# Attention and two MoE layers on one core: the first batch of heads visited twice, and the first MoE block let in earlier

## The chip, the cores and the metric

The kernel runs on one NeuronCore of a Trainium2 chip. The metric is device time of one execution in microseconds (us); smaller is better. Engines are named PE (TensorE matmul), PEld (its weight load), DVE (VectorE), ACT (ScalarE), POOL (GpSimd) and SP (SyncE, which here only issues transfers, one after the other in program order).

## The reference, cut to what matters

Attention over 4 batches, 8 heads, 576 positions of 64 numbers, with a threshold on the scores, then two dense "expert" layers on the 2304 tokens of 512 numbers:

```
scores = (q @ k.T) / 8
thresh = max(scores, axis=-1) - tau
scores = where(scores >= thresh, scores, -1e9)
attn   = exp(scores - max(scores)); attn /= sum(attn) + 1e-9
x      = (attn @ v)                        -> 2304 tokens x 512
layer 1: h = x @ w_in (512 x 2048); g = elu(h);        y = g @ w_out (2048 x 512)
layer 2: h = y @ w_in (512 x 2048); g = max(0.01h, h); y = g @ w_out (2048 x 512)
```

All inputs are float32 and so is the accuracy that is wanted. A product is formed in one of two ways: in plain fp32 on PE, or "split": each operand is written as a high and a low part in the type fp32r, and PE forms high*high, low*high and high*low.

## The kernel before, in words

**Pairs and units.** Two neighbouring heads of one batch make a pair (16 pairs, 4 to a batch), and their 1152 query rows are cut into nine units of 128 rows: A0 to A3 of the even head, B0 to B3 of the odd one, and M, which holds the last 64 rows of both. `ORDER` (L38) is the order in which a pair's units are taken. One unit does: two halves of q.k into a PSUM tile (L488 in fp32, L495 split), the copy to SBUF with the row minimum (DVE, L503), the threshold (L506 or L508), the mask and the exponential on ACT (L512, L515), four PE transposes of the weights (L528) and one shared by two units (L565). The transposed weights are copied out of PSUM by 128 rows at a time: for an fp32 product by two plain copies (`wh`, `lt`, L585 and L587, recorded at L617 on ACT or L618 on DVE), for a split product by a cast on ACT (L595, L602) and a subtraction on DVE (L598, L605) for each of the two. When a head's window of 256 rows (w = 0: units 0 and 1) or 320 rows (w = 1: units 2, 3 and half of M) is full, its attn.v product is formed (`pv32`, L636: five fp32 matmuls; `pv`, L655: nine split ones) and copied into `x` (L641; L661 and, for the split form, a DVE addition, L662). After the ninth unit the row sums are transposed (L538), inverted (L539), sent through DRAM and back (L540, L544), and `x` of that pair is scaled (`scaled`, L550).

**Which heads are fp32.** `Q32` = 4 and `P32` = 9: heads 0 to 3 form q.k, and heads 0 to 8 attn.v, in fp32. An fp32 head has only k, q and v loaded (L404, L405, L392). A split pair goes through `kq_pair` (L417): one load each of the raw k and q of both heads, four POOL operations that split them (L308, L304), and twelve SBUF-to-SBUF transfers (L438) that put the parts where PE wants them. The raw and high tiles have one buffer, `k1` and `k2` two (one for each head of a pair), the q tiles one for each head of a pair. v of a split head is split by two POOL operations (L397 to L399).

**MoE blocks beside the attention.** Layer 1's first half of the hidden dimension (8 slices of 128) is computed for six blocks of 256 tokens while attention runs (`beside`, L835), into the PSUM banks `h` and `y`. Block i needs the scaled `x` of all four pairs of the batches that its tokens lie in (`block_deps`, L831). Each of its eight steps is 12 matmuls of `step_h` (L696) and 12 of `step_y` (L737). The 16 weight tiles that these steps need are loaded (L261) and split on POOL, DVE and ACT at a pace set by `wv0` and `wv1`. While the bank pair is free of blocks (`early`, the first `NS` = 41 units), every second unit's scores go to bank `y` and the shared transpose to `h`; after that all scores go to the one tile `s`. After the 144th unit attention's memory is given back, the second half of layer 1's weights is loaded, and the rest (layer 1's other blocks, then layer 2) runs.

**Order.** All instructions are first listed with their dependences, a cost, and a due time (`vt`): a unit's is its number times `TU`, to which `ST0` (the first `U0` units) or `ST1` adds an offset for each kind of operation; block i's is `bs[i]` times `TU`, and `bdt` for each step. A planner (`Order.run`) then walks through time and puts on each engine, among the operations that its cost model holds ready, the one with the smallest due time. That gives a fixed order for each engine and for SP; on the chip every engine goes through its order and waits where an operand isn't there. SP's model has no bandwidth: 600 ns for each issue, and a latency.

Of the kernel before, what the change touches and what calls it, by code (L numbers as in the profile page):

```python
# [20 lines left out]
NH = B * H  # L21
P32, Q32 = 9, 4
# [15 lines left out]
ORDER = ("A0", "A1", "A2", "A3", "M", "B2", "B3", "B0", "B1")  # L38
COLS = ("A0", "A1", "A2", "A3", "M", "B0", "B1", "B2", "B3")
# [7 lines left out]
ST0 = dict(qk=-10184.2, max=-1817.2, thr=14955.0, exp=-1497.1, mask=5372.6, rec=-38303.7, norm=-27876.4,  # L47
           tr=-1492.3, hi=-17426.6, lo=-14703.9, lhi=28901.5, llo=26005.4, pv=-66898.0)
ST1 = dict(qk=-17406.0, max=4726.7, thr=-9260.7, exp=-6889.7, mask=-5170.3, rec=10649.6, norm=11088.8, tr=5091.6,
           hi=-37131.6, lo=5775.7, lhi=-970.1, llo=-7799.8, pv=-16488.8)  # L50
# [162 lines left out]
def mm32(n):  # L213
    return 2 * (3 + n / 1.2)
# [3 lines left out]
def attn_moe_kernel(ctx, tc, qT, kT, vm, tau, w1i, w1o, w2i, w2o, yp, rsd, out):  # L218
# [36 lines left out]
    def weight(layer, which, f, vt, after=(), reg=False):  # L255
# [6 lines left out]
                after, [raw], vt - 4000, lat=4500)  # L262
# [124 lines left out]
    def head(g, u):  # L387
        vt = (u - KN["hleadb" if g % 2 else "hlead"]) * TU
        par = g % 2
        if g < P32:  # L390
            v = v_r.new(F32)
            ov = op((SP, 600, lambda: nc.sync.dma_start(out=v()[:, :, 0:D], in_=vm[g])), [], [v], vt + KN["vlate"],  # L392
                    lat=3000)
        else:
            vr, v = vraw_r.new(), v_r.new()
            hi, lo = (lambda: v()[:, :, 0:D]), (lambda: v()[:, :, D:2 * D])
            lv = op((SP, 600, lambda: nc.sync.dma_start(out=vr(), in_=vm[g])), [], [vr], vt - 3000, lat=3000)  # L397
# [3 lines left out]
        if g < Q32:  # L401
            k, q = k1_r.new(F32), k2_r.new(F32)
            due = vt - (3e3 if g else 3e4)
            lk = op((SP, 600, lambda: nc.sync.dma_start(out=k()[0:64], in_=kT[g])), [], [k], due, lat=3000)  # L404
            lq = op((SP, 600, lambda: nc.sync.dma_start(out=q()[0:64, 0:S], in_=qT[g])), [], [q], due, lat=3000)  # L405
            heads[g] = (k, k, q, v, (lk, lq), ov)
            if "tau" not in heads:
                heads["tau"] = load_tau(vt)
            return
# [3 lines left out]
        heads[g] = (k1, k2, q, v, deps, ov)  # L413
# [3 lines left out]
    def kq_pair(p, vt):  # L417
# [4 lines left out]
        for r, h, src, n in ((kr, kh, kT, SL), (qr, qh, qT, S)):  # L422
            ld = op((SP, 600, lambda r=r, src=src: nc.sync.dma_start(
                out=r(), in_=src[2 * p:2 * p + 2].rearrange("g d s -> (g d) s"))), [], [r], vt - 3000, lat=3500)
# [5 lines left out]
        for j in range(2):  # L430
# [3 lines left out]
            for dst, at, cs, src, raw, o in (  # L434
# [5 lines left out]
                    [o], [src, dst], vt + 1500 + 5 * TU * j, lat=3000))  # L440
# [6 lines left out]
    def unit(u, p, name):  # L447
# [23 lines left out]
        def er(n=S):  # L471
            return e()[:, side, 0 if side or n > S else 1:n if side or n > S else S + 1]

        def ssr(n=S):
            return ss()[:, 1:S + 1] if n == S else ss()[:, side:side + S + 1]

        nm, thr = (sm_r[t].new() for t in ("nm", "thr"))
        n9 = u % NU
        if n9 == 0:
            sums[p] = (su_r.new(), [])  # L480
        su, col = sums[p][0], COLS.index(name)
        hd = [heads[pc[0]] for pc in pieces]

        def qk32(j):
            for n, (g, c, _, _, w) in enumerate(pieces):
                k, _, q = heads[g][:3]
                c -= 64 if g % 2 and name != "M" else 0
                nc.tensor.matmul(s()[n * w:n * w + w, j, 0:HALF], q()[0:64, c:c + w],  # L488
                                 k()[0:64, k0 + j * HALF:k0 + (j + 1) * HALF], start=True, stop=True)

        def qk(j):
            for n, (g, c, *_) in enumerate(pieces):
                k1, k2, q = heads[g][:3]
                for m, kk in enumerate((k1, k2)):
                    nc.tensor.matmul(s()[:, j, 0:HALF], q()[:, c:c + 128], kk()[:, k0 + j * HALF:k0 + (j + 1) * HALF],  # L495
                                     start=(n == 0 and m == 0), stop=(n == len(pieces) - 1 and m == 1))
# [3 lines left out]
        cost, fn = (mm32(HALF), qk32) if q32 else (2 * mm(HALF), qk)  # L500
# [16 lines left out]
        sums[p][1].append(o)  # L517
        if n9 == NU - 1:
            row_sums(p, vt + so["rec"])
# [11 lines left out]
        turned.append((vt, pieces, t4, t, ott, o, side))  # L531
# [3 lines left out]
    def row_sums(p, vt):  # L535

        (su, done), rb, rt, ps = sums.pop(p), rb_r.new(), rt_r.new(), v_ps.new()
        o = op((PE, 107, lambda: nc.tensor.transpose(ps()[0:NU, 0:128], su(), ident)), done, [su, ps], vt)  # L538
        o = op((DVE, dve(128), lambda: nc.vector.reciprocal(out=rt(), in_=ps()[0:NU, 0:128])), [o], [ps, rt], vt)  # L539
        o = op((SP, 600, lambda: nc.sync.dma_start(out=rsd[p].rearrange("(c p) -> c p", p=128), in_=rt())),  # L540
               [o], [rt], vt, lat=2500)
        got = []
        for a, c, r, n in ((0, 0, 0, S), (64, 0, S + 64, 512), (64, 512, S, 64)):
            got.append(op((SP, 600, lambda a=a, c=c, r=r, n=n: nc.sync.dma_start(  # L544
                out=rb()[a:a + 64, c:c + n], in_=rsd[p, r:r + n].partition_broadcast(64))), [o], [rb], vt, lat=3000))
# [25 lines left out]
    def weights(vt, pieces, t4, t, ott, _, side, lv, otl, so):  # L571
        l0 = 64 * side
        c0 = 0
        for g, _, w, c, n in pieces:
# [9 lines left out]
            if f32:  # L584
# [5 lines left out]
                if full:  # L590
                    pv32(g, w, vt + so["pv"])
# [335 lines left out]
```

## Time and profile before

| | |
|---|---|
| Time, median of 3 runs | 1123.71 us (1123.56 to 1124.15) |
| Profiled execution | 1122.48 us, of which 1120.7 us are the span of its instructions |
| Instructions | 17435 |
| Granted TensorE clock | 1.000 over the span |
| PE: chain that ended last | 91% of the span; DVE 5%, ACT 3% |
| First q.k matmul on PE | 6.4 us |
| Last inversion of row sums of the first batch | 121.3 us |
| First matmul of a MoE block | 138.0 us |
| Last inversion of row sums, end of attention | 443.3 us |

The first 443 us are attention with the six blocks beside it; the remaining 677 us are matmuls of the two layers almost alone. A matmul's recorded length overlaps the next one's, so a matmul's cost is read as the distance from its start to the start of what follows it. An fp32 matmul leaves two records.

### The profile page before, as it was taken

To read this page: it belongs to the slowest core of one execution; us is meant where nothing else is said; L and a number is where in the kernel's file an instruction comes from. 1 tells how busy PE (TensorE), PEld (TensorE's weight loads), DVE (VectorE), ACT (ScalarE), POOL (GpSimd) and SP (SyncE) were. 2 spreads that over 40 slices of the span, in tenths; PEclk is the share of its full clock that TensorE was granted. 3 is DMA by queue.
4 is the path that set the end of the run, shared out by engine and by line. 5 is a ranking of instruction groups with operands and counts; after the bars stand their busy time and mean duration, and the time that the engine had idled before them with its cause. 6 is when DMAs were issued, how large, how long until landed. Compare 5 with 4: busy or idle time off the path is not lost.

```text
span 1120.7 us, 17435 instructions
## 1 busy us (share of the span) xinstructions
PE 1103.0 (98%) x6328; PEld 932.4 (83%) x6328; DVE 712.3 (64%) x1467; ACT 622.3 (56%) x1315; POOL 285.0 (25%) x385
## 2 busy tenths in 40 slices
PE   8999999999999999999999999999999999999998
PEld 4455589999999999889888888988888888888898
DVE  6677798889888887578787784866432332332232
ACT  6778789998888897555455453544322322222232
POOL 4355567565636552012111020100000000000000
PEclk9999999999999999999999999999999999999999
DMA  6466645545454531323442330322010010010010
GB/s 183 112 164 151 168 134 131 160 115 132 115 133 114 132 93 40 95 76 121 143 131 76 113 116 17 114 75 75 1 38 1 1 38 1 1 38 1 1 39 19
DMA packets 50645, 95.45 MB, mean 85 GB/s; under 512 B 13168, under 2 KB 20864, under 8 KB 50560
## 3 DMA queue, kind: packets, MB, share of 16 engines
q1 hardware_dynamic: 50560, 94.34, 29.9%
q8 instruction: 50, 0.82, 0.3%
q14 instruction: 35, 0.29, 0.1%
HBM read 58.20 MB, written 9.51 MB: 60 GB/s over the span
## 4 chain that ended last, share of the span: by engine, by line
PE 91%; DVE 5%; ACT 3%; issue 1%; DVEq 0%; ACTq 0%
PE y L737 34%; PE h L696 19%; PE hb L696 15%; PE v L636 5%; PE s L495 5%; PE v L655 5%; PE t L528 5%; DVE ss L503 1%; ACT e L515 1%; PE s L488 1%; DVE rt L539 1%; PE y L495 1%; PE y L488 1%; DVE wl L598 1%; ACT ss L512 1%
## 5 line engine op out<-in xcount | busy, mean ns | idle before, releaser
L737 PE MATMUL y<-gh,woh 128*128 128x512 f32 (+1 forms) x736 | 257.2, 349 | 1.3 <-DVE ys L618 0.9
L737 PE MATMUL y<-gl,woh 128*128 128x512 f32 (+1 forms) x736 | 252.5, 343 | 0.0
L737 PE MATMUL y<-gh,wol 128*128 128x512 f32 (+1 forms) x736 | 252.2, 343 | 0.0
L696 PE MATMUL h<-xh,wih 128*128 128x256 f32 (+1 forms) x464 | 158.8, 342 | 1.0 <-DVE g L714 1.0
L737 PEld LDWEIGHTS y<-gh,woh 128*128 128x128 f32 x736 | 139.1, 189 | 18.6 <-DVE ys L618 1.4
L696 PE MATMUL h<-xh,wil 128*128 128x256 f32 (+1 forms) x464 | 153.2, 330 | 0.0
L696 PE MATMUL h<-xl,wih 128*128 128x256 f32 (+1 forms) x464 | 153.1, 330 | 0.0
L737 PEld LDWEIGHTS y<-gl,woh 128*128 128x128 f32 x736 | 139.2, 189 | 16.2 <-DVE gl L303 0.2
L737 PEld LDWEIGHTS y<-gh,wol 128*128 128x128 f32 x736 | 139.0, 189 | 16.3
L721 ACT CAST gh<-g 128x512 fp32r<-128x512 f32 (+1 forms) x184 | 97.0, 527 | 91.2 <-DVE g L719 49.0
L512 ACT ACTIVATE ss<-ss,thr 128x576 f32<-128x576 f32 x144 | 111.7, 776 | 19.8 <-DVE thr L508 13.4
L303 DVE TENSOR_TENSOR gl<-g,gh 128x512 fp32r<-128x512 f32 (+1 forms) x129 | 84.2, 652 | 52.8 <-ACT gh L721 51.7
L515 ACT ACTIVATE e<-ss,taun 128x577 f32<-128x577 f32 x144 | 112.2, 779 | 2.5 <-PE h L565 0.8
L503 DVE TENSOR_SCALAR_CACHE_REDUCE ss<-s,scl 128x576 f32<-128x576 f32 x124 | 100.6, 811 | 19.9 <-PE s L495 7.9
L304 POOL TENSOR_TENSOR xl<-x,xh 128x256 fp32r<-128x256 f32 (+1 forms) x32 | 27.9, 884 | 290.3 <-ACT xh L674 290.3
L696 PE MATMUL hb<-xh,wih 128*128 128x512 f32 (+1 forms) x272 | 99.1, 364 | 0.0
L495 PE MATMUL s<-k,qt 128*128 128x288 f32 x512 | 97.8, 302 | 1.3 <-DVE ss L503 1.1
L696 PE MATMUL hb<-xl,wih 128*128 128x512 f32 (+1 forms) x272 | 99.1, 364 | 0.0
L696 PE MATMUL hb<-xh,wil 128*128 128x512 f32 (+1 forms) x272 | 99.0, 364 | 0.0
L696 PEld LDWEIGHTS h<-xh,wih 128*128 128x128 f32 x464 | 87.5, 189 | 10.2 <-ACT lt L602 0.8
L696 PEld LDWEIGHTS h<-xl,wih 128*128 128x128 f32 x464 | 87.7, 189 | 8.5 <-POOL xl L304 0.2
L696 PEld LDWEIGHTS h<-xh,wil 128*128 128x128 f32 x464 | 87.5, 189 | 8.1
(538 smaller groups left out, 1959.8 us busy)
## 6 DMA issues: line engine op xcount, KB each, us to landing
k<-kh SPq DMA_DIRECT2D x56, 160.0 KB, 2.5
k<-kraw SPq DMA_DIRECT2D x56, 160.0 KB, 2.9
wraw<-in_w1i_dram SPq DMA_DIRECT2D x16, 512.0 KB, 3.5
wraw<-in_w1o_dram SPq DMA_DIRECT2D x16, 512.0 KB, 3.5
wraw<-in_w2i_dram SPq DMA_DIRECT2D x16, 512.0 KB, 3.6
wraw<-in_w2o_dram SPq DMA_DIRECT2D x16, 512.0 KB, 3.4
kraw<-in_kT_dram SPq DMA_DIRECT2D x14, 320.0 KB, 3.1
ys<-yp_dram SPq DMA_DIRECT2D x4, 1024.0 KB
```

What stands on the lines that cost most here:

```text
L303: return pick(who, D=(dve(n), lambda: nc.vector.tensor_tensor(**args()), PORT), P=(pool_tt(n), lambda: nc.gpsimd.tensor_tensor(**args())))
L304: P=(pool_tt(n), lambda: nc.gpsimd.tensor_tensor(**args())))
L495: nc.tensor.matmul(s()[:, j, 0:HALF], q()[:, c:c + 128], kk()[:, k0 + j * HALF:k0 + (j + 1) * HALF], start=(n == 0 and m == 0), stop=(n == ...
L503: o = op((DVE, dve(S) + 60, lambda: nc.vector.tensor_scalar(out=ssr().rearrange("p (j c) -> p j c", j=2), in0=s()[:, :, 0:HALF], scalar1=s ...
L512: o = op((ACT, act(S) + 95, lambda: nc.scalar.activation(out=ssr(), in_=ssr(), func=AF.Prelu, bias=thr(), scale=-1.0, alpha=STEEP)), [ot], ...
L515: o = op((ACT, act(S) + 190, lambda: nc.scalar.activation(out=er(S + 1), in_=ssr(S + 1), func=AF.Exp, bias=taun, accum_out=su()[:, col:col ...
L528: nc.tensor.transpose(t4()[:, c, :], er()[:, c1 + c * 128:c1 + (c + 1) * 128], ident)
L636: nc.tensor.matmul(ps()[0:64, 0:nw], lhs, rhs, start=(c == 0), stop=(c == 4))
L655: nc.tensor.matmul(ps()[:, 0:nw], vv()[:, c, :], y()[:, yc, 0:nw] if yc is not None else y()[:, 0:nw], start=(n == 0), stop=(n == 8))
L696: nc.tensor.matmul(hp(), w_()[:, cs], x_()[:, 0:tb], start=(k == 0 and z == 0), stop=(k == KC - 1 and z == 2))
L721: o1 = op((ACT, act(tb), lambda: nc.scalar.copy(out=gh()[:, cs], in_=g()[:, cs])), [o], [g, gh], vt)
L737: nc.tensor.matmul(ysl(yg, m), w_()[:, cs], g_()[:, 0:tb], start=(first and z == 0 and share == 0), stop=(last and z == 2 and end))
```

## The change

The first batch's four pairs are taken in two visits instead of one. `FIRST` does the units A0, A1, B0, B1 of all four pairs (16 units, the first 256 rows of each head, tokens 0 to 255 of the batch), `SECOND` the units A2, A3, M, B2, B3 (20 units, the last 320 rows), and the other twelve pairs are done as before (`ALL`). Each visit loads k, q and v of its heads anew and has its own row sums and its own scaling of `x`; `block_deps` now looks at ranges of tokens, so that block 0 (tokens 0 to 255) needs only the four FIRST visits.

fp32 is left to FIRST: q.k of all eight heads (`Q32` = 20, but only there), attn.v of heads 0 to 4 (`P32` = 5). All SECOND and ALL visits are split. The due times are new: block 0's and block 1's move from 46.325 and 62.85 units to 19.686 and 40, the weights' pace from 4.28 to 3.78 units for a tile, scores leave bank `y` after 16 units instead of 41, and `pv32`'s five matmuls are one operation of the planner.

```diff
-P32, Q32 = 9, 4
+P32, Q32 = 5, 20
-ORDER = ("A0", "A1", "A2", "A3", "M", "B2", "B3", "B0", "B1")
-U0 = H // 2 * NU
-KN = dict(margin=49.6784, pad=30.0, late=1.30757, plead=2.02161, warm=3, TU=2594.9, hlead=-1.09928,
-          hleadb=1.51858, wv0=3.7208, wv1=4.27865, yoff=32778.1, coff=-7939.5, NS=41, vlate=-5075.7,
-          bs=[46.325, 62.85, 80.6, 98.984, 114.51, 134.31], bdt=1.91944, look=0.128169)
+ALL = (("A0", "A1", "A2", "A3", "M", "B2", "B3", "B0", "B1"), ("A0", "A1", "A2", "A3", "M", "B0", "B1", "B2", "B3"),
+       (0, S), ((0, 0, 0, S), (64, 0, S + 64, 512), (64, 512, S, 64)))
+FIRST = (("A0", "A1", "B0", "B1"),) * 2 + ((0, 256), ((0, 0, 0, 256), (64, 0, 256, 256)))
+SECOND = (("A2", "A3", "M", "B2", "B3"),) * 2 + ((256, S), ((0, 0, 0, 320), (64, 0, 384, 256), (64, 256, 320, 64)))
+PLAN = [(p, kind) for kind in (FIRST, SECOND) for p in range(H // 2)] + [(p, ALL) for p in range(H // 2, NH // 2)]
+U0 = H // 2 * len(FIRST[0])
+KN = dict(margin=31.666, pad=0, late=1.30757, plead=2.29704, warm=3, TU=2578.7, hlead=-1.2502, hleadb=1.94318,
+          wv0=3.66401, wv1=3.77649, yoff=31272.0, coff=-12887.2, NS=16, vlate=-1115.6,
+          bs=[19.686, 40, 74.316, 88.029, 111.03, 127.05], bdt=1.92668, look=0.259586)
...
-        if g < P32:
+        if kind is FIRST and g < P32:
             v = v_r.new(F32)
...
-        if g < Q32:
+        if kind is FIRST and g < Q32:
             k, q = k1_r.new(F32), k2_r.new(F32)
...
-        q32, early = ga < Q32, u < KN["NS"]
+        q32, early = kind is FIRST and ga < Q32, u < KN["NS"]
         for g in {"A": (ga,), "B": (gb,), "M": (ga, gb)}[name[0]]:
-            if g not in heads:
-                head(g, u)
+            if (n, g) not in heads:
+                head(n, kind, g, u)
...
-        xready[bt, hp] = [op(tt("DP", S, lambda: dict(out=xs, in0=xs, in1=rb(), op=ALU.mult)),
-                             [*got, *waits.pop((bt, hp))], [rb], vt + 9000)]
+        o = op(tt("DP", hi - lo, lambda: dict(out=xs, in0=xs, in1=rb()[:, 0:hi - lo], op=ALU.mult)),
+               [*got, *waits.pop((bt, hp))], [rb], vt + 9000)
+        xready.setdefault((bt, hp), []).append((bt * S + lo, bt * S + hi, o))
...
-            f32 = g < P32
+            f32 = kind is FIRST and g < P32
...
-    for u in range(NUN):
-        unit(u, u // NU, ORDER[u % NU])
-        if u % NU == NU - 1:
-            scaled(*divmod(u // NU, H // 2))
+    u = 0
+    for n, (p, kind) in enumerate(PLAN):
+        for name in kind[0]:
+            unit(u, n, p, kind, name)
+            u += 1
+        scaled(n, p, kind)
...
-        return [sum((xready[b_, k] for b_ in range(b0, b1 + 1)), []) for k in range(KC)], b1
+        return [[o for b_ in range(b0, b1 + 1) for lo, hi, o in xready[b_, k] if lo < t0 + tb and hi > t0]
+                for k in range(KC)], b1
```

The due offsets `ST0` and `ST1` change too (in SECOND the second set now holds), and the modelled landing times of the transfers are shorter.

## Rows read from the trace of the kernel before

**Rows 1.** Stretches: length, busy us of PE, PEld, DVE, ACT, POOL, clock, DMA share, GB/s.
```profile
0.00:55.00 55.00, 51.77 (x202) 24.73 (x203) 35.07 (x88) 36.11 (x74) 22.26 (x32) 1.00 0.55 150
55.00:121.00 66.00, 65.66 (x316) 36.37 (x314) 48.32 (x109) 49.78 (x106) 33.90 (x45) 1.00 0.62 163
121.00:443.00 322.00, 311.41 (x2427) 296.40 (x2427) 277.04 (x668) 285.25 (x687) 176.44 (x260) 1.00 0.47 121
443.00:1120.00 677.00, 674.14 (x3387) 574.91 (x3385) 351.92 (x604) 251.11 (x452) 52.40 (x49) 1.00 0.17 55
```
**Rows 2.** The same view: the start, all of attention, and the stretch where MoE sets in.
```profile
0.00:6.40 6.40, 4.28 (x6) 1.71 (x6) 1.93 (x10) 1.28 (x1) 0.70 (x6) 1.00 0.54 149
140.00:180.00 40.00, 36.46 (x286) 34.81 (x286) 37.01 (x87) 35.75 (x86) 25.14 (x35) 1.00 0.48 137
0.00:443.00 443.00, 428.83 (x2943) 357.51 (x2944) 360.43 (x863) 371.14 (x864) 232.59 (x336) 1.00 0.50 131
```
**Rows 3.** PE in order of time, fp32 work: start us, length us, line, tiles, records.
```profile
46.01 0.65 PE L528 MATMUL t<-ident,e 128*128 128x128 f32 x4
46.59 0.65 PE L636 MATMUL v<-wh,v 128*64 128x256 f32 x2
47.17 0.75 PE L488 MATMUL y<-k,k 64*128 64x288 f32 x2
...
53.53 1.23 PE L488 MATMUL y<-k,k 64*128 64x288 f32 x4
54.70 0.75 PE L636 MATMUL v<-wh,v 128*64 128x320 f32 x2
55.38 0.66 PE L528 MATMUL t<-ident,e 128*128 128x128 f32 x4
```
**Rows 4.** PE in order of time, split work.
```profile
197.38 0.31 PE L655 MATMUL v<-lt,v 128*128 128x320 f32 x1
197.52 0.69 PE L495 MATMUL s<-k,qt 128*128 128x288 f32 x4
198.05 0.28 PE L696 MATMUL h<-xh,wih 128*128 128x256 f32 x1
...
198.41 0.60 PE L528 MATMUL t<-ident,e 128*128 128x128 f32 x4
198.76 0.36 PE L696 MATMUL h<-xh,wih 128*128 128x256 f32 x1
...
204.56 0.28 PE L655 MATMUL v<-wh,v 128*128 128x256 f32 x1
204.68 0.28 PE L655 MATMUL v<-wl,v 128*128 128x256 f32 x1
```
**Rows 5.** Groups on DVE, 121 to 443 us: count | busy us, mean ns | idle before.
```profile
L598 DVE TENSOR_TENSOR wl<-t,wh 128x512 fp32r<-128x512 f32 (+1 forms) x115 | 71.9, 632 | 11.3 <-ACT wh L595 9.8
L605 DVE TENSOR_TENSOR lt<-t,lt 64x128 fp32r<-64x128 f32 (+1 forms) x114 | 30.7, 275 | 4.3 <-ACT lt L602 1.7
L662 DVE TENSOR_TENSOR x<-v,x 64x320 f32<-64x320 f32 (+1 forms) x45 | 20.5, 455 | 2.7 <-ACT x L617 1.7
L539 DVE RECIPROCAL rt<-v 9x128 f32<-9x128 f32 x12 | 11.3, 941 | 0.2
```
**Rows 6.** SP in order of time: the transfers of one pair's k and q.
```profile
139.31 0.37 SPq L423 DMA_DIRECT2D kraw<-in_kT_dram  x1
...
154.63 0.47 SPq L438 DMA_DIRECT2D qt<-qraw  x1
162.75 1.11 SPq L438 DMA_DIRECT2D k<-kh  x2
...
167.72 0.39 SPq L423 DMA_DIRECT2D kraw<-in_kT_dram  x1
```
**Rows 7.** DVE in order of time: the same shift of 512 numbers, twice.
```profile
87.64 0.42 DVE L270 TENSOR_SCALAR wa__905<-wa__905 128x512 uint32<-128x512 uint32 x1
...
96.06 1.77 DVE L270 TENSOR_SCALAR wa__1008<-wa__1008 128x512 uint32<-128x512 uint32 x1 [0.23 <-POOL wa__1008 L266]
```

More of the change, by code (lines that the diff above doesn't have):

```diff
@@ L445, in attn_moe_kernel, with unit @@
     xready = {}
-    def unit(u, p, name):
+    def unit(u, n, p, kind, name):
         vt = u * TU
@@ L479, in unit @@
[L479 to L482, printed above, removed]
-        def qk32(j):
[L485 to L489, printed above, removed]
+        if name == kind[0][0]:
+            sums[n] = (su_r.new(), [])
@@ L491, in qk @@
+        su, col = sums[n][0], kind[1].index(name)
+        hd = [heads[n, pc[0]] for pc in pieces]
+        def qk32(j):
+            g, c = pieces[0][:2]
+            k, _, q = heads[n, g][:3]
+            c -= 64 * (g % 2)
+            nc.tensor.matmul(s()[:, j, 0:HALF], q()[0:64, c:c + 128], k()[0:64, k0 + j * HALF:k0 + (j + 1) * HALF],
+                             start=True, stop=True)
         def qk(j):
-            for n, (g, c, *_) in enumerate(pieces):
-                k1, k2, q = heads[g][:3]
+            for i, (g, c, *_) in enumerate(pieces):
+                k1, k2, q = heads[n, g][:3]
@@ L530, in unit @@
         ott = op((PE, 4 * 107, tr), [o], [e, t], vt + so["tr"])
-        turned.append((vt, pieces, t4, t, ott, o, side))
+        turned.append((vt, n, kind, pieces, t4, t, ott, o, side))
         if side or name == "M":
             finish(early, e, so)
[L535 to L541, printed above, removed]
-        got = []
-        for a, c, r, n in ((0, 0, 0, S), (64, 0, S + 64, 512), (64, 512, S, 64)):
-            got.append(op((SP, 600, lambda a=a, c=c, r=r, n=n: nc.sync.dma_start(
-                out=rb()[a:a + 64, c:c + n], in_=rsd[p, r:r + n].partition_broadcast(64))), [o], [rb], vt, lat=3000))
-        bt, hp = divmod(2 * p, H)[0], p % (H // 2)
-        xs = x[:, hp, bt * S:(bt + 1) * S]
-        rbs[p] = (rb, got, xs, vt)
@@ L557, in finish, with scaled @@
+    def scaled(n, p, kind):
+        (bt, hp), (lo, hi) = divmod(p, H // 2), kind[2]
+        rb, got, vt = rbs.pop(n)
+        xs = x[:, hp, bt * S + lo:bt * S + hi]
+        o = op(tt("DP", hi - lo, lambda: dict(out=xs, in0=xs, in1=rb()[:, 0:hi - lo], op=ALU.mult)),
+               [*got, *waits.pop((bt, hp))], [rb], vt + 9000)
+        xready.setdefault((bt, hp), []).append((bt * S + lo, bt * S + hi, o))
     def finish(early, e, so):
         lv = (hps_a if early else t_r).new()
[L560 removed]
+        done = list(turned)
@@ L568, in finish, with weights @@
         for d in done:
             weights(*d, lv, otl, so)
-    def weights(vt, pieces, t4, t, ott, _, side, lv, otl, so):
+    def weights(vt, n, kind, pieces, t4, t, ott, _, side, lv, otl, so):
         l0 = 64 * side
         c0 = 0
-        for g, _, w, c, n in pieces:
-            f32 = g < P32
+        for g, _, w, c, rows in pieces:
+            f32 = kind is FIRST and g < P32
             if (g, w) not in wins:
```

125 lines of the change are left out of this document (65 added, 60 removed).

## The prediction, made before the changed kernel was run

> **What bounds the kernel now.** I read busy time by stretches first. After 443 us PE is busy 674 of 677 us [rows 1]: the two layers alone, which the change doesn't touch. What can move is when attention with its six blocks ends. Before 443 us PE is busy 428.8 us and idle 14.2, DVE is busy 360.4 and ACT 371.1 [rows 2]. So PE is the limit there too, but not by much: from 121 to 443 us PE stands at 311.4 of 322 (96.7%) while DVE and ACT together fill (277.0 + 285.3) / 644 = 87.3% [rows 1]. The timeline of PE says what it does in the first 121 us: matmuls start back to back, most of them plain fp32 ones that take about twice a split one's time [rows 3, 4]. The first MoE matmul comes at 138 us, so until then PE is full of attention alone, much of it dear. That is where the change acts.
>
> **PE's work, part by part** (start to start, since recorded ends overlap).
>
> attn.v in fp32: a 256-wide matmul takes 47.17 - 46.59 = 0.58 us, a 320-wide one 55.38 - 54.70 = 0.68 [rows 3], so a window of five takes 2.9 or 3.4. Before: 9 heads with both windows, 9 x 2.9 + 9 x 3.4 = 56.7. After: five windows of 256, 14.5. Split, a matmul takes 0.12 (256) or 0.14 (320) [rows 4], a window of nine 1.1 or 1.3; added are 4 of the first and 9 of the second kind, 16.1. Net -26.1 us.
>
> q.k: an fp32 unit takes 54.70 - 53.53 = 1.17 [rows 3], a split one 198.05 - 197.52 = 0.53, M twice that [rows 4]. fp32 units go from 18 to 16 (M units taken as one unit each, since no row here separates them): -2.3. Split ones: two whole pairs go (10 times 0.53 each), four visits of five units come (6 times 0.53 each): 24 - 20 = 4 times 0.53, +2.1. Net -0.2.
>
> Transposes: four take 0.58 beside fp32 work [rows 3], 0.35 beside split work [rows 4]. The 20 SECOND units now stand among split matmuls: between 0 and -4.6, I take half, -2.3. Four more row-sum transposes: +0.4 at most. Sum for PE: -28.2 us, 400.6 instead of 428.8. The blocks' 6 x 8 x 24 matmuls stay the same; block 0 is only moved.
>
> By the Trainium skill ("FP8 and Floating Point Precision", TensorE Precision Notes) true fp32 is four passes through the array; at 2.4 GHz a 256-wide matmul would then take 0.43 us as an estimate, not 0.58, a 320-wide one 0.53, attn.v would save 16 us instead of 26 and PE's whole sum would be -18. The trace here shows the dearer value, with the switch from one matmul to the next in it, and I keep that.
>
> **What DVE and ACT take over.** A piece of 128 rows of an fp32 head costs two plain copies; a split piece has the same two as casts and two DVE subtractions more, 0.632 + 0.275 us [rows 5]. Pieces in fp32 go from 9 x 4.5 to 5 x 2: 30.5 pieces x 0.907 = 27.7. Each of 13 more split windows has a DVE addition, 0.455: 5.9. Four more inversions of row sums at 0.94: 3.8 [rows 5]. Sum +37 us, all on DVE; copies and thresholds that may run on ACT or POOL let the planner share it out. The pair's work is then 360.4 + 371.1 + 37 = 769 us, 384 for each engine, against 400.6 on PE. The three would be nearly level.
>
> **When attention ends.** FIRST stays bound by PE: 16 x (1.17 + 0.58) + 5 x 2.9 + 3 x 1.1 + small transposes = 47.5 us after the 6.4 us of the start [rows 2, 3], about 55 us with its tail. DVE and ACT do about 80 us there: 71 us in the old first 55 us [rows 1], and I add 9 for a few more units and for six split pieces. Left after 55 us: PE 400.6 - 4.3 (warm-up [rows 2]) - 47.5 = 349, the pair 769 - 80 = 689, or 344.5 each. Bounds from the rows: if PE keeps its 96.7% the rest takes 361 us; if the pair keeps 87.3% it takes 395. The nearest stretch in which all three were loaded alike is 140 to 180 us, PE 91.2%, the pair (37.0 + 35.8) / 80 = 91.0% [rows 2]; by that it takes 379 to 382. That was the moment when MoE set in, with weights still being made, so it is a harsh sample; I take 375, three quarters of the way from 361 to 380. Attention ends at 55 + 375 = 430 instead of 443, -13 us.
>
> Block 0 beside SECOND is what makes this possible: 8 x 24 x 0.12 = 23 us of PE work [rows 4] where PE's own SECOND work is only about 33 (12.7 for q.k, 10.4 for attn.v, some 10 for transposes). If it didn't come, the saved PE time would be idle. SECOND adds transfers: each visit 2 raw loads, 12 copies, 2 of v, 4 for row sums and 1.3 weights, 3.7 MB by their shapes; at 163 / 0.62 = 263 GB/s for full queues [rows 1] that is 14 us in a visit of 5 units of 375 / 128 = 2.95 us, 14.7 us (59 for the four). I cost it at nothing because it fits, but only just.
>
> The single tile `s` from unit 16 on is how later units ran at 96.7% PE already; I cost it at nothing. The later blocks' new due times only order the same work. After the end nothing changes: PE is the cover of all of it.
>
> The profiled execution was 1122.48 us, 1120.7 of span and 1.8 around it, and lies 1.2 under the median; I take the 13 us off the median: 1123.7 - 13 = **1111 us**.
>
> **Rivals.**
> (a) PE stays the limit and the others keep up: 361 us for the rest, end at 416, -27: 1097. For it: 96.7% over 322 us [rows 1]. Against it: the pair would need 344.5 / 361 = 95%, which no stretch in the rows has.
> (b) Slower: the k and q chain of SECOND. It has one raw buffer, and q tiles that are free only when the last visit's unit is done. Before, from the raw load to the last copy for the even head took 154.63 - 139.31 + 0.5 = 15.8 us, and from the odd head's first copy to the next raw load 5.0 [rows 6], 20.8 of the 28.4 us between two raw loads. Strung up as they were, four visits take 4 x 20.8 = 83 us, not 59, +24 us: 1135. It decides from 17.4 us a visit on (+11 in all). For it: SP goes through its list in order, and in `kq_pair` the odd head's copies are due five units after the pair's, a whole visit. Against it: those 15.8 us held waits that had time to spare.
> (c) Weights hold block 0. A step needs two tiles that come every 3.78 units; the last comes at 60 units. If only half of block 0 is done in SECOND, PE works 33 + 11.5 of 59 us there, and the other 304 us of its work at 92.7% need 328: 55 + 59 + 328 = 442, 1122 to 1123: the block is let in but does nothing for the time.
> (d) DVE and POOL get in each other's way. The same shift took 0.42 us and, with POOL at work, 1.77 [rows 7]. SECOND and FIRST add 32 POOL operations (8 for two more split pairs, 24 for twelve more heads' v). If half of them cost DVE 1.35 us, that is +22 on DVE, +11 for the pair's share: 1122. The Trainium skill ("SBUF — State Buffer", Who interferes with whom) has the rule: the two share a port pair, held for a whole instruction, and the loser blocks fully. The trace agrees at that one shift; how often it strikes here no row counts.
>
> **How the numbers follow.** Forecast 0.44 (1103 to 1117 of its own), (a) 0.24, (b) 0.19, (c) 0.07, (d) 0.06. Within 0.2% means 1121.5 to 1126, about what a measurement of this kernel can't tell from no change. Faster: 0.44 + 0.24 = 0.68; same: (c) and (d), 0.13; slower: (b), 0.19. The range goes from (a), 1096, to a mild (b), 1127; it leaves out the worse half of (b) and what lies under 1096.
>
> **What would show it.** L636 falls from 180 records to 50, L488 from 80 to 64, the copies of k from 56 to 64 of each kind. FIRST's last inversion near 55 us, SECOND's last near 114, the last of all near 430. First L696 near 58 us. DVE and ACT together above 90% after 55 us, PE near 93%. If PE is at 96% or more, (a); if PE has gaps between 55 and 114 us that end with the first q.k of a visit waiting for copies, (b); if they end with `step_h` waiting for weights, (c). The prediction is wrong if attention ends after 441 us, or if the time after its end differs from 677 us by more than 3.

## The result: 1139.46 us, slower by 1.4%, and the profile after

The changed kernel takes 1139.46 us (median of 4, 1137.39 to 1140.58) beside 1123.63 us for the kernel before: a ratio of 1.0138 [1.0121, 1.0156]. The forecast was 1111 us, with a range up to 1127. (Ratios here and below leave out runs in which TensorE's clock was down for unusually long.) The profiled execution took 1137.39 us, with 1135.6 us of span, and shows the same loss.

Inversions of row sums mark how far attention has come. The first batch ends at 134.9 us where it ended at 121.2; the first pair that is visited once ends at 172.2 (before 144.2); attention ends at 459.3 (before 443.3). First the stretches between these marks in the kernel before: length, busy us of PE, PEld, DVE, ACT, POOL, clock, DMA share, GB/s.

```profile
0.00:121.20 121.20, 117.44 (x517) 61.10 (x517) 83.59 (x197) 86.09 (x180) 56.36 (x77) 1.00 0.59 157
121.20:144.20 23.00, 22.00 (x116) 13.76 (x116) 17.74 (x46) 19.29 (x42) 12.88 (x18) 1.00 0.59 155
144.20:443.30 299.10, 289.69 (x2313) 282.91 (x2314) 259.10 (x624) 266.05 (x645) 163.35 (x242) 1.00 0.46 118
```

And after, which answers to [rows 1, 2]: FIRST without its tail, SECOND, the first whole pair, the other eleven, and what follows attention.

```profile
0.00:55.00 55.00, 48.71 (x213) 28.64 (x214) 44.12 (x94) 41.27 (x83) 30.49 (x46) 1.00 0.70 195
58.90:134.90 76.00, 62.48 (x404) 57.67 (x404) 63.95 (x145) 59.09 (x139) 51.26 (x65) 0.89 0.73 196
134.90:172.20 37.30, 30.34 (x192) 27.10 (x191) 32.70 (x77) 29.96 (x70) 21.45 (x27) 0.91 0.44 120
172.20:459.30 287.10, 274.81 (x2144) 263.54 (x2145) 252.23 (x622) 254.44 (x608) 137.22 (x206) 1.00 0.46 119
459.30:1135.00 675.70, 670.63 (x3360) 571.87 (x3358) 353.73 (x607) 238.11 (x432) 58.83 (x60) 1.00 0.17 56
```

Three things stand in these rows. The time after attention is what it was. The last eleven pairs run at their old pace, PE at 95.7% (96.9% before), DVE and ACT together at 88.2% (87.8%); they take 287.1 us for 299.1 because block 0's work now comes earlier. The loss is in SECOND and the pair behind it: PE fills 82% there, DVE and ACT together (63.95 + 59.09 + 32.70 + 29.96) / 226.6 = 82%, and the granted clock is 0.89 and 0.91 where it was 1.00. In the kernel before, PE was 97% busy up to this point.

What PE waited for from 58.9 to 172.2 us, longest in total first (line waiting, releaser: us in total, times, longest):

```profile
PE v L661 <- DVE rt L546: 4.6, 4, 1.5
PE s L500 <- DVE ss L508: 4.0, 7, 1.0
PE h L702 <- DVE g L720: 2.6, 2, 2.1
PE t L533 <- ACT ss L517: 2.1, 1, 2.1
PE t L533 <- ACT e L520: 1.5, 4, 0.6
PE t L533 <- DVE wl L605: 1.3, 2, 0.8
```

They end with DVE and ACT, in short pieces at many places, and none with a copy of k or q or with a weight. The first entry is attn.v behind an inversion of row sums, of which the change has four more. The clock is at its lower level in part of this stretch. This is SECOND's attn.v in PE's order of time (start us, length us); [rows 4] had 0.14 us from one 320-wide matmul to the next, here it is 0.27, twice as long, at the lower of the two levels:

```profile
70.42 0.47 PE L661 MATMUL v<-wl,v 128*128 128x320 f32 x1
70.69 0.47 PE L661 MATMUL v<-wh,v 128*128 128x320 f32 x1
70.96 0.47 PE L661 MATMUL v<-wl,v 128*128 128x320 f32 x1
```

DVE's groups up to 459.3 us, which answer to [rows 5] (count | busy us, mean ns):

```profile
L605 DVE TENSOR_TENSOR wl<-t,wh 128x512 fp32r<-128x512 f32 (+1 forms) x150 | 92.7, 629 | 16.9 <-ACT wh L602 14.8
L612 DVE TENSOR_TENSOR lt<-t,lt 64x128 fp32r<-64x128 f32 (+1 forms) x144 | 38.3, 273 | 5.3 <-ACT lt L609 2.2
L668 DVE TENSOR_TENSOR x<-v,x 64x320 f32<-64x320 f32 (+1 forms) x58 | 26.5, 457 | 2.0 <-ACT x L624 0.9
L546 DVE RECIPROCAL rt<-v 9x128 f32<-9x128 f32 (+2 forms) x20 | 18.8, 942 | 0.9 <-PE v L545 0.6
```

The records are 35 large subtractions, 13 additions and four inversions more than before in all of attention (forecast 30.5, 13 and 4), each at its old price: the forecast's terms for this added work stand.

### The profile page after: what moved, and what is told of

The parts are those of the page before. It is cut to its first block, busy times and chain, and to the rows that moved or that the text cites. A ratio compares the mean times of both kernels' runs of the same rounds, so it can differ in the third digit from the quotient of the medians.

```text
span 1135.6 us, 17672 instructions
## 1 busy us (share of the span) xinstructions
PE 1088.5 (96%) x6319; PEld 949.9 (84%) x6319; DVE 750.6 (66%) x1549; ACT 625.9 (55%) x1337; POOL 301.0 (27%) x404
## 4 chain that ended last, share of the span: by engine, by line
PE 73%; ACT 7%; DVE 6%; issue 2%; POOL 1%; DMA 0%; POOLq 0%; DVEq 0%; ACTq 0%
PE y L743 32%; PE h L702 17%; PE hb L702 14%; PE v L661 4%; PE s L500 3%; ACT e L520 2%; PE t L533 2%; ACT ss L517 2%; ACT wh L602 2%; DVE ss L508 1%; DVE wl L605 1%; DVE lt L612 1%; ACT lt L609 1%; DVE rt L546 1%; DVE g L720 0%
## 5 line engine op out<-in xcount | busy, mean ns | idle before, releaser
L727 ACT CAST gh<-g 128x512 fp32r<-128x512 f32 (+1 forms) x184 | 97.0, 527 | 91.8 <-DVE g L725 52.0
L500 PE MATMUL s<-k,qt 128*128 128x288 f32 x576 | 109.6, 306 | 6.7 <-DVE ss L508 5.9
L508 DVE TENSOR_SCALAR_CACHE_REDUCE ss<-s,scl 128x576 f32<-128x576 f32 x136 | 110.1, 810 | 8.5 <-PE s L493 2.9
L605 DVE TENSOR_TENSOR wl<-t,wh 128x512 fp32r<-128x512 f32 (+1 forms) x150 | 92.7, 629 | 16.9 <-ACT wh L602 14.8
L533 PE MATMUL t<-ident,e 128*128 128x128 f32 x576 | 90.3, 280 | 9.9 <-DVE wl L605 4.5
```

The source lines that it names most:

```text
L508: o = op((DVE, dve(S) + 60, lambda: nc.vector.tensor_scalar(out=ssr().rearrange("p (j c) -> p j c", j=2), in0=s()[:, :, 0:HALF], scalar1=s ...
L533: nc.tensor.transpose(t4()[:, c, :], er()[:, c1 + c * 128:c1 + (c + 1) * 128], ident)
L605: nc.vector.tensor_tensor(out=wl()[:, :, dst], in0=t4()[:, :, src], in1=wh()[:, :, dst].bitcast(F32), op=ALU.subtract)
L727: o1 = op((ACT, act(tb), lambda: nc.scalar.copy(out=gh()[:, cs], in_=g()[:, cs])), [o], [g, gh], vt)
```

## The experiments

The expectations name these theories. **Load**: DVE and ACT, given the work of the split heads, set SECOND's time. **Chain**: the transfers of k and q for the second visits do. **Crowding**: block 0, let in at 16 units, is in the way. **Clock**: PE waits, falls to its lower clock, and that is the loss. **Tune**: the order of the kernel before fits the chip unusually well, and any kernel planned anew loses that. Each kernel ran on the same chip as runs of the kernel before (medians 1123.9 to 1124.2 us); the numbers in brackets are the ratio to it with its 95% interval. "Planned anew" means that the planner saw other operations, costs or due times, so that the engines' orders changed too.

**Giving arithmetic back to PE.** In the changed kernel, attn.v of SECOND goes back to plain fp32 for all heads (first), and q.k too (second). The edit is written here in short; the kernels do it through two helper functions.

```
-        if kind is FIRST and g < P32:
+        if g < (P32 if kind is FIRST else 8 if kind is SECOND else 0):     # v: plain
...
-        if kind is FIRST and g < Q32:
+        if kind is FIRST and g < Q32 or kind is SECOND and g < 8:          # k, q: second kernel only
```

> The changed kernel with attn.v of all eight heads back in plain fp32 in the SECOND visits (q.k stays split). PE gets 8 x (3.4 - 1.3) = 17 us more there, DVE about 20 pieces x 0.9 + 8 x 0.5 = 22 us less, POOL about 10 less. Theory Load (DVE and ACT are too full in the first batch, PE starves beside them): SECOND, 58.9 to 134.9 us in the changed kernel, shrinks by 8 to 11 us, attention ends near 450, time 1129 to 1132. Theory Chain (SECOND waits for its k and q transfers): SECOND stays within 2 us of 76, time 1138 to 1141. Theory Clock (PE, with gaps, falls to the lower of its two clock levels and that costs the 17 us that its busy time is over the forecast): more PE work keeps the clock up, granted clock from 60 to 140 us goes from about 0.89 to above 0.97, and the time falls further than the DVE load explains, under 1128.

Measured: 1141.47 us (1.0132 [1.007, 1.0194]). SECOND takes 73.0 us and the first whole pair 32.5, together 7.8 less; FIRST's end came 8.8 later (67.7 us), with the clock down in its first 40 us. Only some 3 of the 7.8 are the lighter DVE's: the changed kernel's own order, when FIRST ends late, has 73.1 and 35.4 (under "The start"). Less work on DVE did not make the kernel faster.

> As the run before, and q.k of the SECOND visits in plain fp32 too, so that the first batch needs no split k and q: 48 copies and 16 POOL operations fewer, 15 us more on PE. Theory Chain: SECOND falls from 76 to about 60 us, time 1122 to 1126, most of it in the step from the run before to this one. Theory Load: the step from the run before is small, within 3 us, since DVE and ACT have the same work; POOL's relief may give 2 us, PE's 15 us take as much.

Measured: 1152.98 us (1.0226 [1.0172, 1.0281]), SECOND 78.5 us. Its stretch from 60 to 140 us (columns as above):

```profile
60.00:140.00 80.00, 74.34 (x391) 49.01 (x391) 58.93 (x135) 54.47 (x120) 35.83 (x43) 0.94 0.40 113
```

The queues are at 0.40, with no k or q copies of SECOND left, and SECOND is no shorter, which Chain had put at about 60 us. PE has much more fp32 work in it, though, and is busy for 74 of the 80 us, so this kernel alone doesn't settle it; together with the list of PE's waits above, where no copy stands, Chain falls.

**Holding the block.** The changed kernel with the early blocks' old due times.

```
-NS=16 ... bs=[19.686, 40, 74.316
+NS=41 ... bs=[46.325, 62.85, 80.6
```

> The changed kernel with block 0 and block 1 due where the kernel before had them (46.325, 62.85, block 2 at 80.6 units) and with scores alternating between two tiles for the first 41 units: two visits and the split arithmetic, without the early block. Theory Crowding (block 0 and its operands beside SECOND are what slows SECOND): SECOND falls to 62 us or less and the time to 1125 or below. Theory Load: SECOND gains the some 10 us of DVE and ACT work that block 0 had there, but PE then has nothing to fill its gaps, and its 23 us come back later: 1138 to 1148, and the granted clock under 0.85 in SECOND.

Measured: 1151.08 us (1.0212 [1.0161, 1.0264]). SECOND took 69.4 us, and PE had even less to do:

```profile
60.00:140.00 80.00, 55.34 (x303) 48.93 (x302) 66.30 (x158) 58.10 (x136) 48.89 (x60) 0.83 0.77 207
```

DVE is as busy as with the block (67.73 us in the same stretch of the changed kernel). Crowding falls: SECOND is some 4 to 7 us shorter without the block, but not 62, and the block's work comes back later.

**The arithmetic alone.** The kernel before, one visit a pair, with attn.v of two heads instead of nine in fp32.

```
-P32, Q32 = 9, 4
+P32, Q32 = 2, 4
```

> The kernel before with attn.v in fp32 for heads 0 and 1 only (four windows of 12.6 us instead of eighteen of 56.7): nearly the arithmetic of the changed kernel, in one visit and with block 0 where it was. Theory Load: PE has 28 us less to do in the first batch, DVE and ACT some 40 more, and nothing fills PE; the time is not lower than before, 1122 to 1135, and PE idle in the first 138 us grows from 5 to over 20 us. If PE's work were what counts (my forecast's view), it would fall to 1105 to 1112. Theory Chain or Crowding: neither is touched, so the loss of 16 us must not show here: 1124 or below.

Measured: 1143.40 us (1.0167 [1.0098, 1.0237]), the same loss without any second visit. The stretch looks like the changed kernel's:

```profile
60.00:140.00 80.00, 55.50 (x289) 46.91 (x289) 66.76 (x138) 61.40 (x137) 44.57 (x60) 0.83 0.52 141
```

PE's fp32 work, taken away, left PE idle for 24.5 of 80 us, and the kernel slower. This speaks for Load, though the size is past what Load gave, and this kernel is planned anew too, which by itself can move the time (below).

**The start.** PE waits for head 1's k at about 9 us, 1.13 us in the changed kernel's profile, where the clock holds, and 2.1 to 3.3 in five others, where it is then at the lower level for some 14 to 17 of the first 40 us. First: its k and q asked for earlier, in the changed kernel and in the one with attn.v of SECOND in fp32.

```
-            due = vt - (3e3 if g else 3e4)
+            due = vt - (3e3 if n or g > 1 else 3e4)
```

> The changed kernel with the loads of head 1's k and q due at the very start, ahead of the first weight tile and of the pair loads of SECOND (one due time changed, nothing else). In the changed kernel the first q.k of head 1 waits 1.1 us for them, and in the first and third run of the experiments 3.3 and 2.9 us, after which PE ran at its lower clock until the first inversion came at 30.7 and 28.8 us instead of 22.0. Theory Start (FIRST needs its second head after two units and a late load costs more than its own wait, through the clock): the wait goes, the first inversion comes at 20 to 22 us, and the time falls by 1 to 4 us, to 1135 to 1138. Theory Load (where the 16 us go is DVE and ACT after 59 us): no more than that.

> The first experiment (attn.v of SECOND in plain fp32) with the same early loads, so that its start is that of the changed kernel. Theory Load: the 8 us that the first experiment gained between 59 and 200 us now show in the time: 1129 to 1133. Theory Clock or Chain: they expect no other number here, since PE's work and the transfers are those of the first experiment; a time at 1140 would say that the loss of its start was not a late load but moves around.

Measured: 1139.42 us (1.0127 [1.0087, 1.0168]) and 1138.64 us (1.0119 [1.0078, 1.0159]). The edit missed: SP issued head 1's k at 4.88 us as before, behind some 1.5 MB, and PE waited 2.08 us. The first of the two is useful all the same. Its engines go through the changed kernel's order, so its profile is a second execution of that kernel, with another course of the clock. FIRST ends at 64.8 us; then SECOND and the first whole pair, with the same numbers of instructions as above, take 73.1 and 35.4 us:

```profile
64.76:137.88 73.12, 59.02 (x404) 53.68 (x404) 63.75 (x145) 58.91 (x139) 51.60 (x65) 0.95 0.76 205
137.88:173.29 35.41, 27.68 (x191) 24.04 (x191) 33.22 (x77) 29.85 (x70) 21.34 (x27) 1.00 0.45 125
```

PE is at its lower level for some 7 us here, where it was 23 in the changed kernel's profile, and the two stretches are 4.8 us shorter: 0.3 us for each us at that level. That is an upper estimate, since a FIRST that ends later also gives the transfers behind it more time.

**More work on PE.** The changed kernel with split attn.v of SECOND and of the first whole pair formed twice, 15 us of PE.

```
+        reps = 2 if H // 2 <= n <= H else 1
...
-        for r in range(0, 9, 3):
+        for r in range(0, 9 * reps, 3):
```

> The changed kernel with every split attn.v product of the four SECOND visits and of the first whole pair after them formed twice, the second over the first: 8 x 1.3 + 4.8 = 15 us more PE work between 60 and 172 us, no more work for any other engine. Theory Clock (gaps on PE lower its clock, and that is what costs the time): the granted clock between 60 and 180 us rises from 0.90 to 0.97 or more and the time stays within 2 us or falls. Theory Load: PE has room there, about 28 us of gaps between 60 and 172, but attn.v stands among the rest in program order: the time rises by 0 to 8 us, to 1140 to 1147, and the clock follows PE's busy share. If PE were the limit there, the time would rise by all 15: 1154.

Measured: 1141.29 us (1.0134 [1.0088, 1.018]). The clock of 140 to 180 us rose from 0.91 to 1.00 and that of 60 to 140 from 0.89 to 0.96; 15 us of work cost about 2. In the profile SECOND took 80.4 us (76.0), so some of the added work does show there, and the eleven pairs behind were 3.8 us shorter. This kernel is planned anew; what it shows is that a clock back at 0.96 to 1.00 does not by itself bring the time back.

**Is it the order?** Constants of the planner moved a little, with the work unchanged: three times in the kernel before, twice in the changed one. (The padding is added to each ACT, DVE and POOL instruction; an expectation calls it that of matmuls, which is wrong.)

```
-pad=30.0 / margin=49.6784         -pad=0, / margin=31.666
+pad=29.0, pad=31.0 / margin=48.0  +pad=1.0, / margin=33.0
```

> The kernel before with one constant of the planner's cost model changed by a little (29 instead of 30 ns added to each operation of ACT, DVE and POOL): the same work in a slightly other order. Theory Tune (the orders are fitted to one kernel each, and any change of the work or of a cost loses 10 to 20 us whatever it does): 1130 or more. Theories Load, Start and Clock: the orders of similar plans are alike, 1121 to 1128.

> The kernel before with its padding of matmuls in the planner at 31 instead of 30 ns: the same work in a slightly other order. Theory Tune (the order of before is a fitted one, and any kernel that is planned anew loses it): slower than before by 5 to 20 us, 1129 to 1144, as the 29 ns did (1137.6). Theory Load (the change's own added DVE and ACT work sets its time): within 4 us of before, 1120 to 1128, since no work is added.

> The kernel before with another constant of the planner moved a little (margin 48 for 49.68). As for the 31 ns: by theory Tune 1129 to 1144; by theory Load 1120 to 1128. The two together with the 29 ns give the spread of the old work over small changes of its order.

> The changed kernel with its padding at 1 instead of 0 ns: the same work in a slightly other order. Theory Tune: if the changed kernel's order is itself a fitted one it loses 5 to 20 us here, 1144 to 1159; if it is an ordinary one it moves by 5 us either way, 1134 to 1145. Theory Load: 1136 to 1143. Slower than the perturbed kernels before by about as much as its own work costs.

> The changed kernel with margin 33 for 31.67. As with the padding: by theory Tune 1144 to 1159 for a fitted order, 1134 to 1145 for an ordinary one; by theory Load 1136 to 1143. If the two perturbed changed kernels are level with the three perturbed kernels before, the change's work costs nothing by itself and the whole loss is of the order.

| kernel | median us | ratio | runs at a clock of 0.998 or more |
|---|---|---|---|
| before, pad 29 | 1137.62 | 1.008 [1.0046, 1.0113] | 1128.96 to 1129.58 |
| before, pad 31 | 1121.48 | 0.9975 [0.9935, 1.0014] | 1120.20 to 1121.53 |
| before, margin 48 | 1124.02 | 0.9987 [0.996, 1.0013] | 1123.63 to 1125.63 |
| changed, pad 1 | 1157.15 | 1.0256 [1.0192, 1.032] | none |
| changed, margin 33 | 1149.44 | 1.0189 [1.0125, 1.0252] | none |

I had taken the first row for a sign of Tune; the next two, level with the kernel before, refute it as a rule. At full clock the old work keeps its time within 6 us over small changes of its order. By medians its four orders lie between 1121.5 and 1137.6 us, the three of the changed work between 1139.5 and 1157.2, and no run of those reached full clock; the tested version is the best of its three. How much of the difference is the order and how much the work can't be read from so few.

The runs of one kernel also give the clock's price. With pad 31, ten runs fall into three groups: 1120.2 to 1121.5 us at a mean clock of 1.000, 1130.0 at 0.991, 1140.8 to 1140.9 at 0.981. The profile of one of the last (columns as above):

```profile
13.00:52.00 39.00, 39.00 (x90) 16.88 (x90) 16.09 (x41) 17.86 (x37) 9.47 (x15) 0.50 0.27 79
52.00:60.00 8.00, 8.00 (x24) 3.26 (x22) 2.19 (x6) 3.04 (x8) 1.66 (x2) 0.68 0.00 1
```

PE, full all the time, is at the lower level for some 43 us, and the run is 20 longer: 0.46 us lost for each us there, where PE is the limit; the middle group, some 20 us at that level and 9 longer, agrees. The changed kernel's runs have mean clocks of 0.984 to 0.990, so 23 to 36 us at the lower level in every run. At 0.46 that would be 10 to 17 us, at the 0.3 from above 7 to 11. The few runs each of the changed kernel and of those that keep its order give 0.13 to 0.36 by their own spread.

**Holding the start, and removing work.** The changed kernel with head 1's k and q right behind head 0's and three matmuls as filler before unit 2; the same without SECOND's low halves; the same with attn.v twice. The filler:

```
+        if u == 2:
+            def fill():
+                for _ in range(3):
+                    nc.tensor.matmul(s()[:, 0, :], wz[:, 1:129], wz[:, 1:513], start=True, stop=True)
+            hdeps = [*hdeps, op((PE, 900 * 3, fill), [], [s], vt + so["qk"] - 1)]
```

> The changed kernel with head 1's k and q requested right behind head 0's and three fp32 matmuls of 512 columns (about 2.6 us, their result overwritten) put on PE before the third unit, so that PE does not wait there. Theory Clock (most of the loss is PE running at its lower clock after waits, 0.9 us for each us at that level): the granted clock of the first 60 us is 1.00 in every run, the kernel comes out at 1130 to 1135, and what is left of the loss is the lower clock of 60 to 180 us. Theory Load (DVE and ACT carry more): 1137 to 1143, since the first 60 us are not what the added pieces lengthen.

> As the start-filled kernel, and of the second visits DVE's subtractions that form the weights' low halves are left out (24 instructions, 14.0 us of DVE in the changed kernel's trace; PE multiplies the high half twice in their place, so that its work is unchanged). Theory Load: the second visits shorten by 8 to 14 us and the kernel comes out that much below the start-filled one. Theory Clock: below 4 us, unless the granted clock of 60 to 140 us rises to 0.98 or more.

> The start-filled kernel with attn.v of the second visits and of the first whole pair formed twice, 15 us of PE work more. Theory Clock: the clock holds near 1.00 throughout, and the time comes out at 1128 to 1136, level with the start-filled kernel or below it although PE does more. Theory Load: the added work is hidden under DVE and ACT for the most part: 2 to 6 us above the start-filled kernel.

Measured: 1163.59 us (1.0328 [1.0277, 1.0379]), 1136.47 (1.0095 [1.007, 1.0121]) and 1152.51 (1.0226 [1.0166, 1.0285]). Both theories missed the first by over 20 us: the clock held for the first 20 us, was 0.89 from 20 to 40, and the new order was worse throughout. The second is 27 us below the first, where Load gave 8 to 14; the third has more work than the first and is 11 us shorter. A kernel with this structure can move by 10 to 20 us when it is planned anew, so none of the three prices an engine.

**One engine lighter, the order kept.** So the last three keep the order of every engine's instructions and leave out part of one engine's work. DVE: low halves on 8 of 128 columns. PE: the four matmuls on the low half left out. ACT: mask and exponential on 64 of 576 columns. All in SECOND alone.

```
+                if kind is SECOND:                                   # DVE
+                    src, dst = slice(src.start, src.start + 8), slice(dst.start, dst.start + 8)
...
+                if y is wl and H // 2 <= n < H:                      # PE
+                    continue
...
-            out=er(S + 1), in_=ssr(S + 1), func=AF.Exp
+            out=er(S + 1)[:, 0:64] if cut else er(S + 1), ...        # ACT, and the mask alike
```

> The changed kernel with every engine's order kept as it is; in the second visits DVE's subtraction of the weights' low halves is done on 8 of each 128 columns only, and attn.v reads the high half in its place (about 10 of its 14.0 us are left out; the instructions stay in their places). Theory Load (the second visits are bound by DVE and ACT together): 4 to 10 us faster than the changed kernel, 1129 to 1135. Theory Clock (bound by PE at its lower clock): within 3 us, 1136 to 1142.

> The changed kernel in its own order, with attn.v's four matmuls on the low half left out of the nine of each group in the second visits (13.3 us of PE, 36 of 72 matmuls in 60 to 140 us). Theory Load: within 3 us of the changed kernel, 1136 to 1142, or slower if the added idle time lowers the clock further. Theory Clock: PE's work there is what ends last, 8 to 13 us faster, 1126 to 1131.

> The changed kernel in its own order, with ACT's two passes over the scores (the mask and the exponential, 0.78 us each) done on 64 of 576 columns in the second visits: 40 instructions at about 0.43 us less, some 17 us of ACT left out. Theory Load: 6 to 15 us faster, 1124 to 1133, and the lower clock's share falls. Theory Clock: within 3 us, 1136 to 1142. If neither this nor the lighter DVE nor the lighter PE alone moves the time, the second visits are bound by the round of single instructions through the engines and not by the sum of any of them.

Measured: 1137.56 us (1.0104 [1.0065, 1.0143]), 1139.58 (1.0118 [1.008, 1.0156]) and 1138.05 (1.0109 [1.0073, 1.0146]): none moves the time by over 2 us. Left out were some 10 us of DVE and 17 of ACT. For PE the expectation's 13.3 us is too much: by the edit it is 32 matmuls (four of nine in eight windows), and at 0.14 to 0.27 us from start to start that is 4 to 9 us. In the profiles SECOND takes 72.2, 71.6 and 71.8 us, and the first whole pair 35.4 in all three. The changed kernel's profile has 76.0 and 37.3, but there FIRST ended 3 to 6 us earlier; its order with a late FIRST has 73.1 and 35.4 with nothing left out. So 1 to 1.5 us show, or up to some 4 if the clock is allowed for at 0.3 (0.90 to 0.93 in SECOND here, 0.95 there), whichever engine was relieved. The stretch of 60 to 140 us, first with DVE lighter:

```profile
60.00:140.00 80.00, 65.45 (x437) 60.76 (x437) 61.72 (x159) 63.58 (x149) 54.61 (x70) 0.91 0.78 210
```

With PE lighter:

```profile
60.00:140.00 80.00, 62.81 (x406) 56.35 (x406) 71.67 (x159) 64.54 (x151) 56.51 (x70) 0.91 0.77 212
```

With ACT lighter (48 us instead of 61):

```profile
60.00:140.00 80.00, 64.40 (x436) 59.40 (x437) 70.62 (x160) 48.02 (x150) 54.70 (x68) 0.94 0.78 209
```

And the chain that ended last (start us, us, what). With DVE lighter it runs through ACT here, by the same instructions as in the changed kernel, where they start at 120.41 us:

```profile
120.81 0.78 ACT ss L517
121.59 0.27 ACT g L716
121.86 0.75 ACT e L520 x2
122.61 0.48 ACT wh L602
123.09 0.52 ACT woh L294
```

With ACT lighter, through DVE, and the weights' preparation stands in it:

```profile
81.27 0.94 DVE rt L547
82.22 0.28 DVE g L721
82.49 0.73 DVE ss L508 x2
83.22 0.80 DVE wa__915 L276
84.12 0.69 DVE wb__983 L280
84.85 0.48 DVE x L626
```

What the three show is that neither DVE's work nor ACT's nor PE's, each alone, sets SECOND's length; they are 84, 78 and 82% full there in the changed kernel. The reading that fits is that each unit has to pass through all of them in an order that was fixed ahead, and that where one is relieved the next one's queue holds the unit up. That is argued, not shown: POOL, 67% full, and the transfers were not relieved, nor two engines at once, and with ACT lighter one wait for a copy of k (2.96 us) stands in the chain.

## Why the prediction was wrong

**PE's work: nearly right, and worth nothing.** The records fell as counted (attn.v in fp32 to 50, q.k to 64). PE's recorded busy time up to the end of attention fell by 11.3 us only (429.13 to 417.87); matmuls at the lower clock make up to 12 us of the difference (24 us at that level in this execution), which leaves some 5 of the 28.2 us unaccounted for. The arithmetic-alone kernel speaks against any worth of the saving in itself: it is slower by 19 us, though planned anew.

**DVE and ACT: the counted work right, the sum 2% short.** Forecast 769 us, measured 396.83 + 387.79 = 785. The subtractions, additions and inversions came to +39 us on DVE (forecast 37). That DVE as a whole got +36.4 is partly luck: its plain copies of attention's weights fell by 18 us, with ACT taking the casts in their place (+15 for casts and copies together), and its steps on the MoE weights grew by 6.6 (32.0 to 38.6). ACT got 16 us more, a sharing that I had not priced. For the part after FIRST I had 689 us and the trace shows 692; the missing work lies in FIRST, 92 us instead of 80.

**FIRST: 55 us forecast, 58.9 measured**, and it varies: the other profiles without an edit of the start have 62 to 70, after the wait for head 1's k that no step of mine had. I counted PE's matmuls and assumed that a head's k is there when its first unit comes; with two units a head, head 1 is needed after two units instead of four.

**The step that failed: "I take 375, three quarters of the way from 361 to 380".** The rest took 400.4 us. The work was there as summed, so it is the pace: 86.5% for DVE and ACT instead of the 92% that 375 us ask for, PE at 91.8% with its slower matmuls in it. Of the 29.3 us between 430 and 459.3, FIRST holds 3.9, SECOND 17.0 (76.0 instead of 59), the twelve whole pairs 8.4 (324.4 instead of 316). I had the right bound in hand, 395 us if the pair keeps 87.3%, which gives 1131, and left it out of the range as well. That bound holds most of the miss: at 87.3% the measured 692 us of work take 397 us, 22 of the 25 us, and the whole pairs did run at 87.8%. One average over all of the rest also hid SECOND: DVE and ACT were busy for 123 us there, which in 59 us would be 104% of the two. At 87.3% it takes 70.5 us; at the 81% that it had, 76. The 91% of 140 to 180 us, which I called a harsh sample, was a mild one: there MoE matmuls fill PE while only the last of the 16 weights are made, and the clock is 1.00. SECOND has attention's short units, weights' preparation and a block's activations on DVE and ACT at once.

**Block 0 as filler: right, and not enough.** It ran beside SECOND (first matmul 63.0 us, its store 173.7, before 138.0 and 204.0), and holding it back costs 12 us more by one kernel, though that one was planned anew. But PE still stood idle there for 13.5 of 76 us: part of the saved PE time was idle all the same.

**Rivals.** (a) falls: PE is at 91.8% after FIRST, and the lighter PE gains nothing. (b) named the place and came near the time (1135) by another mechanism. Its raw loads of k did come further apart than its threshold of 17.4 us, as SP's order of time shows, which answers to [rows 6]:

```profile
75.58 0.37 SPq L429 DMA_DIRECT2D kraw<-in_kT_dram  x1
...
99.02 0.33 SPq L429 DMA_DIRECT2D kraw<-in_kT_dram  x1
...
117.31 0.33 SPq L429 DMA_DIRECT2D kraw<-in_kT_dram  x1
...
136.21 0.34 SPq L429 DMA_DIRECT2D kraw<-in_kT_dram  x1
```

18 to 23 us, but they follow the visits: none of the listed waits of PE in SECOND ends with a copy, and SECOND without the copies is as long, though with more fp32 work. (c) falls: no step waits for weights there. (d) was not tried by itself, but the trace gives its size: one kind of weight step on DVE grew from 594 to 875 ns on average, and all three kinds by 6.6 us over attention, where (d) had 22; DVE's subtractions, its copies of scores and its inversions keep their lengths in SECOND.

**What stays open.** How the 15.8 us divide between the lower clock, the order, and the passage through the three engines. The clock's part is at most 10 to 17 us by the price that holds where PE is the limit, and 7 to 11 by the 0.3 that two executions of the changed order give. It may be smaller still in SECOND, since 4 to 9 us of PE work less moved the median by 0.1 us; that is argued, not shown. Nor is it shown why DVE and ACT reach 81% in SECOND and 88% later, or why two visits with much fp32 (the first, second and sixth kernel) don't come back to 1124: their start was late, and PE's clock fell at other places.

## What to carry to other kernels

When an edit takes work off the engine that is the limit and gives it to two that are 87% full, price the new stretch by the pace that those two have shown, not by the sum of work over a hoped-for share; with three engines loaded alike in a fixed order, 82 to 88% was what came out here. An engine that is full all the time also hides the others' waits: with its "dear" fp32 matmuls at the start PE was 97% busy up to 144 us, without them 82% in SECOND. Before one kernel's few per cent are explained, move a constant that changes only the order: here that alone moved medians by up to 14 us for the old work (6 at full clock) and 18 for the changed. And before a stretch of a relieved kernel is compared, look for a second execution of the unrelieved one: SECOND took 76.0 us in one and 73.1 in another with the same order.

## What the runs showed of the hardware

One list of instructions gave three times, 1120.2 to 1121.5, 1130.0 and 1140.8 us, by how long the clock was at its lower level. In the profiled one it fell after gaps of 0.27 and 0.85 us on PE, which the kernel before has at the same place (0.26 and 0.85) while its clock holds; PE was then full at the lower level from 13 to 52 us before the clock came back. Why the same gaps cost the clock in one run and not in another, no run shows. One shift of 512 numbers on DVE, 0.42 us at its shortest, took up to 1.49 us in the changed kernel (1.77 before). And 1 ns in the planner's cost of each instruction of ACT, DVE and POOL moved the kernel before, in runs at full clock, between 1121 (31 ns), 1124 (30) and 1129 us (29).
